# A transducer front end and joint network: a leading tile of 384 outputs, a new load order, and weight sums on other engines

## The chip, the cores and the metric

The kernel runs on one NeuronCore of one Trainium2 chip. A core has five engines that run side by side: TensorE (PE in the profile; its weight loads are shown apart as PEld), VectorE (DVE), ScalarE (ACT), GpSimd (POOL) and SyncE (SP), which here issues DMA transfers. They share an on-chip memory of 128 partitions (SBUF); TensorE writes its products into PSUM, eight banks of 512 fp32 columns a partition. Engines wait for each other through semaphores. The metric is the device time of one execution in microseconds (us); lower is better.

## The reference

Two batches of 4000 steps with 512 channels. A convolution over time with five taps and a 512x512 matrix for each tap, then gelu, then every second step; the same again; then a joint network that adds a projection of each of the 1000 remaining steps to each of eight label vectors, takes tanh and multiplies by a 512x512 matrix. All inputs and the output are bf16.

```python
xp = jnp.pad(x, ((0,0),(2,2),(0,0)))                     # x: (2, 4000, 512)
h = sum(jnp.einsum("btc,cd->btd", xp[:, i:i+4000], w1[i]) for i in range(5))
h = gelu(h)[:, ::2]                                       # (2, 2000, 512)
...                                                       # the same with w2: f is (2, 1000, 512)
fe = jnp.einsum("btd,de->bte", f, w_f)
ge = jnp.einsum("bud,de->bue", g, w_g)                    # 8 label vectors
j = jnp.tanh(fe[:, :, None] + ge[:, None])
return jnp.einsum("btud,dv->btuv", j, w_o)                # (2, 1000, 8, 512)
```

## The kernel before

Channels lie on the partitions: 512 channels are four blocks of 128, so each tap is 4 input blocks by 4 output blocks of 128x128 weights, and time runs along the free dimension. A product is one `matmul` (line 412) of a 128x128 weight block with a run of time steps. Odd outputs of the stride-2 convolution are never computed.

**The leading tile.** The first 2 x `NA` = 408 outputs of batch 0 are computed directly: five taps, 80 products of 408 columns (`direct`, line 691), in the order of taps 0, 4, 2, 1, 3. Tap 0 is cut into two halves of two input blocks each, and tap 4's weights are loaded in two halves, so that work can start early. The x rows for this tile come by two plain loads (`xr`, 128 and 78 rows of four steps) and are transposed by TensorE against an identity matrix into PSUM (`turn`, line 489; 32 transposes); VectorE and ScalarE copy them to `xs`, where four rows hold the four phases of x modulo 4 that the taps pick from. Before x arrives, eight products of 512 columns on a zero tile run on TensorE (`warm_mm`); the zero tile is written by VectorE and is also what the identity matrix is made from.

**The triples.** All other outputs are computed three at a time with fewer products than taps times outputs (`Triple`, line 562, and `Unit`). For each group of columns, one column standing for three outputs, there are nine products (`t2`, `tm`, `sm`, `t1`, `s1`, `t0`, `s0`, `ti`, `si`) of four input blocks each. Their inputs are sums of six phases of x (x modulo 6), made by the steps `d2 d1 d0 t2 r2 r1 tm sm r0 t1 s1 prev s0 next t0 ti si` on ScalarE and VectorE; their weights are sums of taps. The first convolution has four such groups: two for the rest of batch 0 (`N3` = 266 and 266 columns) and two for batch 1 (334 each); the second has two of 334. The six phases come by DMA transposes ("turned" loads, `load_x6`) into `xq` and `xp`.

**The weight sums.** `w1part` (line 542) makes, for each output block of 128, w0+w4-w2, w0+w4+w2 and w0+2 w2+4 w4, the first and the last scaled by a third, and for each pair of blocks w1-w3, w1+w3 and 2 w1. Sums are done on VectorE in fp32 SBUF tiles (`ssum`), scalings on ScalarE.

**The units.** A unit is one output block of one group. It runs its nine products into one of five PSUM banks (4, 5, 6, 7, 3, then 0 to 2 when the leading tile has left them); between products ScalarE copies partial results to `sd`, VectorE combines them in a second bank, and ScalarE writes the gelu.

**The joint stage.** 16000 rows of 512 are multiplied by w_o as a 2x2 block scheme with seven products instead of eight (`Seven`), 31 groups of four 128-row tiles, and one last tile as a plain product in two halves (`end`). ScalarE makes the tanh rows, VectorE and GpSimd make sums of them (`ss`), VectorE and ScalarE bring the products out of PSUM into `sn` and into an output tile `og` of four rows, of which there are three; SP stores them. The two halves of the last tile are stored from ScalarE's queue.

**What sets the order.** The program first lists 1711 operations with what they read and write. The order on each engine is not that of the list: it is a table (`ORDER`, line 69), five strings in which two characters are an operation's number, found beforehand by a planner from assumed costs (the numbers given with each operation; `wire` is the assumed duration of a transfer). Where an operation may run on several engines (`flex`) the table also chooses the engine. Waits follow from the reads and writes. An engine does its work strictly in that order, and the SP queue issues transfers in that order too. A transfer can be given a gate, another load whose landing it waits for:

```python
for i, part, gate in ((0, (lo, al), None), (0, (hi, al), None), (4, (slice(0, NK), slice(0, D // 2)), None),
                      (4, (slice(0, NK), slice(D // 2, D)), 0), (2, None, 1), (1, None, 3), (3, None, 5)):
    load_w1(i, part, gate)
for ph in (4, 0, 2, 1, 3, 5):
    load_xq(0, ph)
```

## Time and profile before

| | us |
|---|---|
| median of three runs | 248.97 (248.63 to 248.98) |
| span of the profiled execution | 247.2 |
| what lies around it (median less span) | 1.77 |
| TensorE busy in the span | 242.8 |
| VectorE, ScalarE, GpSimd busy | 224.8, 210.7, 83.8 |
| first warm-up product, first product of the leading tile | 1.19, 7.37 |

The profiled execution was not timed by itself; its span runs from the first to the last instruction, and the rows of the table set it beside the median of the timed runs. In the profile a row of a timeline is: start, duration, engine, line, operation, output <- inputs, form (partitions x elements), count, and in brackets the idle time of the engine before it and what ended it. A row of the chain of waits is start, duration, what. In a windows row each engine has its busy time and count, then come TensorE's granted clock, the busy share of the DMA engines and GB/s. Products overlap, so the time from one start to the next is what a product costs, and its listed duration is longer. A group row has a count, busy time, mean duration in ns, and idle time before it.

### The profile page before, as it was taken

How to read it: one execution, taken by the hardware profiler on the slowest of the kernel's cores; microseconds unless marked ns; L12 is line 12 of the kernel's file. 1: busy time of each engine (PE TensorE's matmuls, PEld its weight loads, DVE VectorE, ACT ScalarE, POOL GpSimd, SP SyncE). 2: the span in 40 equal slices, each digit the busy share in tenths (PEclk: the TensorE clock that was granted, in tenths of full speed). 3: DMA queues.
4: the chain of work that ended last, by engine and by line, in shares of the span. 5: the costliest groups of instructions: out<-in, count | busy, mean ns of one | idle time of the engine just before them, and what ended most of it. 6: DMA issues, size and time to landing. Idle time of an engine off the chain costs nothing.

```text
span 247.2 us, 5277 instructions
## 1 busy us (share of the span) xinstructions
PE 242.8 (98%) x1932; PEld 186.1 (75%) x1932; DVE 224.8 (91%) x403; ACT 210.7 (85%) x359; POOL 83.8 (34%) x90
## 2 busy tenths in 40 slices
PE   8999999999999999999999999999999999999995
PEld 4657888877666666666567888778788888888883
DVE  1799998867999999699998999999999999999994
ACT  3269799899669857986799999999999999999992
POOL 1000000000000000000015584677887886796861
PEclk9999999999999999999999999999999999999999
DMA  6998999997700340000000234413433655356377
GB/s 215 331 193 168 185 157 205 150 177 174 254 2 3 119 135 3 1 1 3 0 0 3 85 102 139 143 48 129 131 127 103 195 171 172 132 187 200 123 258 233
DMA packets 57890, 31.87 MB, mean 129 GB/s; under 512 B 33835, under 2 KB 57659, under 8 KB 57865
## 3 DMA queue, kind: packets, MB, share of 16 engines
q1 hardware_dynamic: 57577, 31.41, 48.5%
q8 instruction: 15, 0.25, 0.4%
q10 hardware_dynamic: 288, 0.13, 0.2%
q14 instruction: 10, 0.08, 0.1%
HBM read 7.66 MB, written 16.38 MB: 97 GB/s over the span
## 4 chain that ended last, share of the span: by engine, by line
PE 98%; DVE 0%; issue 0%
PE acc L412 97%; PE acc L496 1%; DVE ost L835 0%; DVE xs L505 0%; DVE zero L419 0%
## 5 line engine op out<-in xcount | busy, mean ns | idle before, releaser
L398 DVE TENSOR_TENSOR og<-acc,sn 128x512 bf16<-128x512 f32 x93 | 60.0, 690 | 1.9 <-PE acc L412 1.2
L412 PE MATMUL acc<-tw,ss 128*128 128x256 f16 x372 | 58.0, 273 | 0.0
L404 ACT ACTIVATE jT<-feT,geT 128x1000 bf16<-128x1000 f32 (+6 forms) x56 | 53.2, 1002 | 1.8 <-DVE feT L398 1.5
L834 ACT ACTIVATE sn<-acc 128x512 f32<-128x512 f32 (+1 forms) x70 | 43.0, 707 | 1.0 <-PE acc L412 0.7
L412 PEld LDWEIGHTS acc<-tw,ss 128*128 128x128 f16 x372 | 36.0, 98 | 6.5 <-ACT sn L834 0.2
L903 POOL TENSOR_TENSOR ss<-jT 128x512 f16<-128x512 bf16 x24 | 27.7, 1168 | 25.0 <-DVE feT L398 22.5
L412 PE MATMUL acc<-row,w_sb 128*128 128x334 bf16 (+1 forms) x192 | 31.7, 296 | 0.0
L412 PE MATMUL acc<-wo_sb,jT 128*128 128x256 bf16 x176 | 29.2, 273 | 0.0
L404 ACT ACTIVATE sd<-acc 128x334 f32<-128x334 f32 (+1 forms) x48 | 20.6, 435 | 10.1 <-PE acc L412 9.6
L412 PE MATMUL acc<-row,w_x 128*128 128x266 bf16 (+1 forms) x192 | 28.4, 291 | 0.0
L404 ACT ACTIVATE jX<-feT,geT 128x1000 bf16<-128x1000 f32 (+4 forms) x28 | 27.4, 1042 | 0.0
L394 POOL MEMSET hT<- 128x8 bf16 (+2 forms) x6 | 0.7, 149 | 70.5 <-ACT hT L404 70.5
L412 PEld LDWEIGHTS acc<-row,w_sb 128*128 128x128 bf16 x192 | 18.7, 98 | 6.3
L412 PEld LDWEIGHTS acc<-row,w_x 128*128 128x128 bf16 x192 | 18.7, 98 | 5.7
L903 POOL TENSOR_TENSOR ss<-jT,ss 128x512 f16<-128x512 bf16 x14 | 16.6, 1189 | 15.1 <-DVE ss L903 9.7
L412 PE MATMUL acc<-wo_sb,ss 128*128 128x256 bf16 x124 | 21.0, 273 | 0.0
L412 PEld LDWEIGHTS acc<-wo_sb,jT 128*128 128x128 bf16 x176 | 17.2, 98 | 3.1
L835 DVE COPY sn<-acc 128x512 f32<-128x512 f32 (+1 forms) x25 | 16.8, 691 | 1.1 <-PE acc L412 1.0
L412 PE MATMUL acc<-hT,w_sb 128*128 128x334 bf16 x96 | 17.1, 305 | 0.0
L518 DVE SCALAR_TENSOR_TENSOR acc<-acc,sd 128x334 f32<-128x334 f32 (+1 forms) x24 | 11.7, 487 | 5.8 <-PE acc L412 5.6
L404 ACT ACTIVATE hT<-acc 128x266 bf16<-128x266 f32 (+2 forms) x36 | 14.6, 433 | 2.7 <-PE acc L412 2.4
L834 ACT ACTIVATE og<-acc 128x512 bf16<-128x512 f32 x22 | 15.3, 710 | 1.5 <-PE acc L412 1.5
(113 smaller groups left out, 502.5 us busy)
## 6 DMA issues: line engine op xcount, KB each, us to landing
out_dram<-og SPq DMA_DIRECT2D x45, 256.0 KB, 2.3
w_sb<-in_w_dram SPq DMA_DIRECT2D x8, 512.0 KB, 4.9
out_dram<-og SPq DMA_DIRECT2D x19, 128.0 KB, 2.2
w_sb<-in_w_dram SPq DMA_DIRECT2D x4, 256.0 KB, 4.8
xr<-in_x_dram SPq DMA_DIRECT2D x1, 512.0 KB, 3.5
wf_sb<-in_w_f_dram SPq DMA_DIRECT2D x1, 512.0 KB, 3.6
wg_sb<-in_w_g_dram SPq DMA_DIRECT2D x1, 512.0 KB, 5.1
wo_sb<-in_w_o_dram SPq DMA_DIRECT2D x1, 512.0 KB, 5.2
```

The source lines that it names most:

```text
L394: pl.op("pool", lambda e: e.memset(v.ap, 0.0), (), (v,))
L398: pl.op(eng, lambda e: e.tensor_tensor(out=o.ap, in0=a.ap, in1=b.ap, op=op), (a, b), (o,), 0.02 + 2.14e-3 * o.ap.free_size() if eng == "po ...
L404: pl.op("act", lambda e: e.activation(o.ap, i.ap, func, scale=scale, bias=0.0 if bias is None else bias.ap), rd, (o,), o.ap.free_size() * ...
L412: ins = e.matmul(o.ap, lhsT=l.ap, rhs=r.ap, start=start and n == 0, stop=stop and n == len(pairs) - 1, skip_group_check=not check)
L496: ins = e.transpose(pv.ap[:, i, k, :], xr[rt].h[0:n, 2 * r + pp, k, :], ident.h[0:n, 0:n])
L518: pl.op(eng, lambda e: e.scalar_tensor_tensor(out=o.ap, in0=a.ap, scalar=f, in1=b.ap, op0=ALU.mult, op1=add), (a, b), (o,), vec_cost(o, (a ...
L834: pl.flex({"act": (lambda e: e.activation(o.ap, v.ap, ACT.Copy), 0.05 + n * 0.833e-3), "dve": (lambda e: e.tensor_copy(out=o.ap, in_=v.ap) ...
L835: "dve": (lambda e: e.tensor_copy(out=o.ap, in_=v.ap), 0.065 + n * 1.04e-3)}, (v,), (o,))
L903: fn = lambda e, o=S[i], x=x, y=y, op=op: e.tensor_tensor(out=o.ap, in0=x.ap, in1=y.ap, op=op)
```

## The change

- The leading tile has 384 outputs instead of 408 (`NA` = 192), so the second plain x load has 66 rows; the two groups after it have 206 and 334 columns instead of 266 and 266, and `xq` is sized for the larger one. The turned loads have 224 and 336 columns instead of 272 each.
- The loads on SP: after tap 1 come the turned phases 4 and 0 of the first group, then tap 3, then the other four phases. Tap 3's gate is the first half of tap 4 instead of the second.
- Warm-up products read a constant of the preamble (ones) instead of the zero tile, and the identity matrix is made from a constant; the zero tile and VectorE's write of it are gone.
- Weight sums: ScalarE copies tap 4's block into a PSUM bank, and w0+2 w2+4 w4 is formed there by VectorE. For blocks 0 and 1 w0+w4 also stands in PSUM; for blocks 2 and 3 GpSimd forms w0+w4 and its two sums in SBUF. All four blocks stand in the list ahead of the first group's steps, the sums of w1 and w3 behind them, and those may run on VectorE or GpSimd.
- Copies that scale (steps `d`, `next`, `prev`, and the two `sd` copies of a unit) may run on ScalarE or VectorE (`scaled`).
- The products of the leading tile are no longer kept in the order of the list. The new table runs taps 2 and 1 mixed, and puts tap 3 last with the first `t2` product of the first group ahead of it and two more in between.
- Five output tiles `og` instead of three. The stores of the last group and of the last tile may go on SP's or ScalarE's queue: the table puts two half tiles of the last group and both halves of the last tile on ScalarE's. At the end, the last group's last product comes ahead of both halves of the last tile.
- `ORDER` is new throughout (1718 operations). In it 82 of the partial sums of the joint and feature stages run on GpSimd, 71 before.

```diff
-    NA, N3 = 204, (266, 266)
+    NA, N3 = 192, (206, 334)
...
-        xq = [Buf(nc, f"xq{i}", [6, NK, (288, 288)[i]], BF16, v.end - v.bytes) for i, v in enumerate((xs[1], w2_sb))]
+        xq = [Buf(nc, f"xq{i}", [6, NK, (352, 352)[i]], BF16, v.end - v.bytes) for i, v in enumerate((xs[1], w2_sb))]
...
+        og += [at(f"og{i}", [4, NT], BF16, og_off + (i - 3) * 4096) for i in range(3, 5)]
...
-        pl.op("dve", lambda e: e.memset(zv.ap, 0.0), (), (zv,))
...
-                              (4, (slice(0, NK), slice(D // 2, D)), 0), (2, None, 1), (1, None, 3), (3, None, 5)):
+                              (4, (slice(0, NK), slice(D // 2, D)), 0), (2, None, 1)):
             load_w1(i, part, gate)
-        for ph in (4, 0, 2, 1, 3, 5):
-            load_xq(0, ph)
+        for kind, i in (('w', 1), ('x', 4), ('x', 0), ('w', 3), ('x', 2), ('x', 1), ('x', 3), ('x', 5)):
+            if kind == "w":
+                load_w1(i, None, len(came) - 4)
+            else:
+                load_xq(0, i)
...
+            one = [nc.const_aps.tensor(1.0, [P, k], BF16) for k in (P, NT)]
             for _ in range(n):
-                mm(o, [(z, zz)], True, True)
+                pl.op("pe", lambda e: e.matmul(o.ap, lhsT=one[0], rhs=one[1], start=True, stop=True), (), (o,))
...
+        WBANK = ((6, 7), (5, 4), (6, 7), (5, 4))
+        WHOME = ('P', 'P', 'G', 'G')
+
+        def scaled(o, i, f):
+            n = o.ap.free_size()
+            fast = not i.psum and o.ap.dtype == BF16 and i.ap.dtype == BF16
+            pl.port = fast
+            pl.flex({"act": (lambda e: e.activation(o.ap, i.ap, ACT.Copy, scale=f), n * 0.833e-3 + (0.05 if i.psum else 0.105)),
+                     "dve": (lambda e: e.tensor_scalar_mul(out=o.ap, in0=i.ap, scalar1=f), 0.065 + n * (0.26e-3 if fast else 1.04e-3))}, (i,), (o,))
...
         def w1part(m, part):
...
+            home = WHOME[m]
+            if home != "S":
+                u, t = (ps.cols(bk * NT, NT).map(lambda a: a.rearrange("p (k c) -> p k c", k=NK)) for bk in WBANK[m])
+                act(u, w(4), ACT.Copy)
+                w4 = u
...
+            if home == "G":
+                t, v = ssum[4][:], ssum[m % 2][:]
+                tt("pool", t, w(0), w(4), add)
+                tt("pool", v, t, w(2), sub)
+                tt("pool", w1_t[2, :, sl], t, w(2), add)
+            else:
+                v = t if home == "P" else ssum[m % 2][:]
+                tt("dve", t, w4, w(0), add)
+            stt("dve", u, w4, 4.0, w(0))
+            stt("dve", u, w(2), 2.0, u)
+            act(w1_x[1, :, sl], u, ACT.Copy, scale=1.0 / 3.0)
+            if home != "G":
+                tt("dve", w1_t[2, :, sl], t, w(2), add)
                 tt("dve", v, t, w(2), sub)
+            act(w1_x[0, :, sl], v, ACT.Copy, scale=1.0 / 3.0)
+
+        def w13part(m):
+            n = slice(m * P, (m + 2) * P)
+            shared(w1_x[2, :, n], w1_sb[1, :, n], w1_sb[3, :, n], sub, True)
+            shared(w1_t[0, :, n], w1_sb[1, :, n], w1_sb[3, :, n], add, True)
+            scaled(w1_t[1, :, n], w1_sb[1, :, n], 2.0)
...
-                act(self.c, self.pa(), ACT.Copy, scale=1.5)
+                scaled(self.c, self.pa(), 1.5)
...
+        pl.pin = False
         for i in taps:
...
+        def either(o):
+            o.alt = {"sp": (o.fn, 0.43), "act": (o.fn, 0.43)}
...
-        end.half(0, None, "act")
+        end.half(0, None, None)
         seven[-1].p4()
-        end.half(1, None, "act")
+        end.half(1, None, None)
```

145 lines of the change are left out of this document (69 added, 76 removed).

## The prediction

> **What bounds the kernel now.** I read the page's busy times first, then the chain of waits, then TensorE's timeline.
>
> ```profile
> span 247.2 us, 5277 instructions
> PE 242.8 (98%) x1932; PEld 186.1 (75%) x1932; DVE 224.8 (91%) x403; ACT 210.7 (85%) x359; POOL 83.8 (34%) x90
> ...
> 6.99 0.33 DVE xs L505
> ...
> 7.37 236.76 PE acc L412 x1892
> ...
> 244.15 0.42 DVE ost L835
> ```
>
> The chain is TensorE from 7.37 to 244.13 us without one other engine in it. Ahead of it stands a head of 7.37 us (zeros on VectorE, eight warm-up products, transposes, one eviction), behind it a tail of 247.2 - 244.13 = 3.07 us. So three things can move the time: the head, the length of the product stream, and stalls that a new order makes. Whether the stream is dense shows in runs of equal products:
>
> ```profile
> 21.67 1.54 PE L412 MATMUL acc<-xs,w_sb 128*128 128x408 bf16 x8
> 23.05 2.88 PE L412 MATMUL acc<-row,w_x 128*128 128x266 bf16 x24
> 25.77 2.88 PE L412 MATMUL acc<-xq,w_t 128*128 128x266 bf16 x24
> ...
> 71.44 0.73 PE L412 MATMUL acc<-row,w_sb 128*128 128x334 bf16 x4
> 72.01 0.73 PE L412 MATMUL acc<-xp,w_sb 128*128 128x334 bf16 x4
> ```
>
> From start to start: 408 columns (23.05 - 21.67)/8 = 172.5 ns, 266 columns 2.72/24 = 113.3 ns, 334 columns 0.57/4 = 142 ns. The line through the first two is 0.417 ns a column plus 2.5 ns, and gives 141.7 for the third. There is no stall in it to win back: the 80 + 144 products of the first stages already stand back to back.
>
> **The product stream.** The leading tile goes from 408 to 384 columns in 80 products: 384 gives 162.5 ns, so 80 x 10 = -0.80 us. The two column blocks of the first batch go from 266 and 266 to 206 and 334, with 144 products each: 206 gives 88.3, 334 gives 141.7, so 144 x (88.3 + 141.7 - 226.7) = +0.48 us. Net -0.32 us, on the path in full.
>
> The 206-column product is shorter than any long run shown so far, and each needs its own weights:
>
> ```profile
> L412 PEld LDWEIGHTS acc<-row,w_x 128*128 128x128 bf16 x192 | 18.7, 98 | 5.7
> ...
> 100.92 0.25 PE L412 MATMUL acc<-gT,wg_sb 128*128 128x16 bf16 x4
> 101.02 0.44 PE L412 MATMUL acc<-row,w_t 128*128 128x334 bf16 x2
> ```
>
> A weight load lasts 98 ns, yet four 16-column products with four full loads pass in 0.10 us, 25 ns each: loads follow each other much closer than they last. So 88.3 ns stands. The Trainium skill (TensorE: Matmul & The Clock Gate, Back-to-back issue gap) speaks against it: it says that in a real stream of load and product pairs the spacing is set by both, about 81 ns at 128 columns and 131 at 512. An estimate on the straight line between those two is 91 ns at 206, which would add 0.4 us; the same line gives 117 ns at 408 columns, where this trace has 172.5, so the trace does not agree.
>
> **The head.**
>
> ```profile
> 0.86 0.27 DVE L419 MEMSET zero<- 128x256 uint32 x1 [0.86 <-PEq L1221]
> 1.19 3.59 PE L412 MATMUL acc<-zero 128*128 128x512 bf16 x8 [1.19 <-DVE zero L419]
> 4.27 0.10 PEld L496 LDWEIGHTS acc<-ident,xr 128*128 128x128 bf16 x1 [0.40 <-DMA xr<-in_x_dram]
> 4.58 2.66 PE L496 MATMUL acc<-ident,xr 128*128 128x128 bf16 x32
> ...
> 4.57:6.27 1.70, 1.70 (x16) 1.00 1.03 305
> 6.27:6.78 0.51, 0.51 (x11) 1.00 1.15 333
> 6.78:7.06 0.28, 0.28 (x12) 1.00 1.21 298
> ...
> 6.99 0.92 DVE L505 COPY xs<-acc 128x312 bf16<-128x312 bf16 x2 [0.89 <-PE acc L496]
> ```
>
> The warm-up products wait for VectorE's zeros until 1.19 and run to 4.58, 0.42 us each. With a constant of the preamble as operand they start when the engines do, about 0.86: a gain of 0.33 on their own. But the first transpose also needs x, which lands at 4.27, and the products then end at 4.25; I let the transposes start at 4.33, 0.25 earlier. Sixteen of 128 columns take 1.70 us (106 ns each, half speed by the line above: 55.8; the granted clock, third column of the windows, reads 1.00 all the same). The next eight, of 78 columns, take 0.51 to 6.78, still at half speed; with 66 columns 8 x 55 = 0.44, another -0.07. Only the last eight (0.28) run at full speed. The eviction that releases the first product has 312 elements a row, 0.33 us in the chain, and shrinks with 264 to 0.29. Sum -0.36: the direct products start at 7.0. Bounds: 0 if x lands 0.3 later, -0.45 if the transposes start with x's landing and the fast clock comes a little earlier too.
>
> **Loads: tap 3 behind two turned phases.** One queue (SP) issues everything. Now tap 1, tap 3, then the six phases; after, tap 1, phase 4, phase 0, tap 3, the rest. Three answers on DMA issues, one transfer each (tap 1 issued at 7.08, tap 3 at 8.83 as the second of the same row, phase 4 at 9.24, phase 0 at 10.98), and SP's timeline:
>
> ```profile
> w_sb<-in_w_dram SPq DMA_DIRECT2D x1, 512.0 KB, 5.1
> w_sb<-in_w_dram SPq DMA_DIRECT2D x1, 512.0 KB, 4.8
> xq<-in_x_dram SPq DMA_TRANSPOSE x1, 5.4
> xq<-in_x_dram SPq DMA_TRANSPOSE x1, 6.1
> ...
> 7.08 2.12 SPq L430 DMA_DIRECT2D w_sb<-in_w_dram  x2
> 9.24 1.70 SPq L445 DMA_TRANSPOSE xq<-in_x_dram  x1
> 10.98 2.56 SPq L445 DMA_TRANSPOSE xq<-in_x_dram  x1
> ```
>
> They land at 12.2, 13.6, 14.6 and 17.1: the shares are 1.4 us for a tap, 1.0 and 2.5 for the two phases. The phases shrink from 272 to 224 columns. So after: tap 1 12.2, phase 4 13.0, phase 0 15.1, tap 3 16.5; at the old phase sizes 17.1. SP reaches tap 3's issue at 7.45 + 1.70 + 2.56 = 11.7 at the latest, so the issue is not what is late. TensorE asks for tap 3 after 64 direct products and one group of the triples: 7.0 + 64 x 0.1625 + 4 x 0.088 = 17.8. Cost 0, with 0.7 to 1.3 us to spare. The gate on tap 3 (half of tap 4 landed) is past long before. The phases behind tap 3 land about 1.5 us earlier than now, since they are smaller.
>
> **Weight sums off VectorE's SBUF operands.** Per output block VectorE now does five sums and ScalarE two scalings. After, ScalarE also copies tap 4 into a PSUM bank (four copies); VectorE keeps five sums on PSUM operands for two blocks and two for the other two, whose three remaining sums go to GpSimd.
>
> ```profile
> 7.99 0.69 DVE L398 TENSOR_TENSOR ssum<-w_sb 128x512 f32<-128x512 bf16 x1
> ...
> 10.77 0.69 DVE L518 SCALAR_TENSOR_TENSOR ssum<-w_sb,ssum 128x512 f32<-128x512 bf16 x1 [0.88 <-DMA w_sb<-in_w_dram]
> 11.38 0.69 DVE L398 TENSOR_TENSOR ssum<-ssum,w_sb 128x512 f32<-128x512 f32 x1
> ...
> 13.90 1.15 ACT L404 ACTIVATE w_x<-ssum 128x512 bf16<-128x512 f32 x2 [1.20 <-DVE ssum L518]
> 18.00 0.72 DVE L398 TENSOR_TENSOR row<-xq 128x1064 bf16<-128x1064 bf16 x1
> 18.62 0.69 DVE L518 SCALAR_TENSOR_TENSOR ssum<-w_sb,ssum 128x512 f32<-128x512 bf16 x1
> ...
> L903 POOL TENSOR_TENSOR ss<-jT 128x512 f16<-128x512 bf16 x24 | 27.7, 1168 | 25.0 <-DVE feT L398 22.5
> ```
>
> A 512-element sum is 0.61 from start to start on VectorE, 0.57 on ScalarE, 1.17 on GpSimd; a row sum of 1064 is 0.62, so about 0.50 at 824. PSUM sums with two operands are not in this stage; I take 0.60, between that and the full 0.69. VectorE's first sum starts at 7.99 now, when tap 4's first half is in; with ScalarE's copy ahead it begins at about 8.65 and does in the new order eleven sums (15.25), the first row difference (15.75; phase 0 in at 15.1), three sums (17.5), w1-w3 (18.1), five row steps (20.6), x3-x1 (21.1), x1+x3 (21.6), two more of w1 and w3 (22.8). TensorE wants the first difference at 17.4, x3-x1 at 22.2, the last at 23.9. Everything is 1.0 us or more ahead: cost 0. GpSimd's six sums are 7.0 us; even if all wait for tap 2, which is in by 10.77, they are out by 17.7, and products use them from 22.9 on. At 0.69 a sum, fourteen sums lose 1.3 us and the cover is gone.
>
> **The rest.** The page's waits, a group of the same line on ScalarE's queue, landings, windows, and one stall:
>
> ```profile
> DVE og L398 <- PE acc L412: 1.2, 3, 0.5
> ...
> L849 ACTq DMA_DIRECT2D out_dram<-ost x2: 338/358/378, 244.0 to 244.6; - x2
> ...
> out_dram<-ost ACTq DMA_DIRECT2D x2, 64.0 KB, 2.0
> ...
> 180.00:200.00 20.00, 20.00 (x181) 17.20 (x179) 20.00 (x39) 20.00 (x32) 16.39 (x15) 1.00 0.42 136
> ...
> 241.23 0.33 PEld L412 LDWEIGHTS acc<-tw,jT 128*128 128x128 bf16 x4 [0.19 <-DVE og L398]
> ```
>
> Five output buffers: what writes `og` waits for products today (1.2 us), not for a store, so two more buffers gain 0. Last stores: the chain's end stays product, VectorE eviction 0.42, issue on ScalarE's queue, 2.0 to landing. That queue now carries four stores instead of two at 0.36 each; the one ahead of the last is released one half product (0.44 us) earlier, so it is out in time: 0, between -0.36 and +0.36. The scalings that a planner may now give to VectorE, the warm-up's other operand and the earlier identity matrix cost nothing: their engines have waited for products or x there.
>
> The order of every engine after 30 us is new. I cannot cost it row by row. In the joint stage VectorE and ScalarE are busy for all 20 us of 20, so a bad place costs one late eviction, 0.2 us (the stall shown); a good one removes two such at the end, about -0.1 once the overlap of the weight load is taken off. The order moves eleven of VectorE's partial sums to GpSimd, which has room. Taken: 0, ends -0.2 and +1.0 (five such places).
>
> **Sum.** 247.2 - 0.36 - 0.80 + 0.48 = 246.5 us for the span. The median of the three runs, 248.97, stands 1.77 above the profiled span; I keep that: 248.3 us. Within the forecast the head's and the tail's bounds give 247.8 to 248.7.
>
> **The rivals.** What a measurement of this kernel can tell from no change is about 0.2%, 0.5 us: 248.47 to 249.47.
>
> *Tap 3 late (slower).* Place: the first product of tap 3, at 17.8. The order is fixed, so TensorE stands while the load is out, us for us, and w1-w3 and w1+w3 on VectorE move with it. For: phase 0 alone takes 6.1 us from issue to landing, and if tap 3 took that from 11.7 it would land at 17.8 exactly. Against: it takes 4.8 now, and the shares give 16.5. The gain of 0.68 is gone with a landing at 18.5; from 19.0 it is slower. With 19.7, 1.9 late, the time is 250.2.
>
> *The operands of the first triples late (no change).* Banks 4 to 7 hold sums until ScalarE's scalings, and ScalarE takes its work strictly in order, behind copies that wait for x. For: at 0.69 us a PSUM sum the 1.0 us of room is overdrawn by 0.3, and a phase that lands late holds up all of ScalarE's queue behind its copy. Against: VectorE had the same stage full before without one stall of TensorE. Price 0.2 to 1.1 us: about 249.0.
>
> *The fast clock comes earlier (faster still).* The trace has it at 6.78, 5.6 us after the first product, whatever the reason. If 0.33 us more of early products bring it in by 4.3, the transposes lose 16 x 0.051 + 8 x 0.025 = 1.0 us; the first weights, which land at 6.3 to 6.5 (a load like tap 1's issued at 1.7), cap the gain at 0.6: 247.7. Against: nothing in the trace shows a shorter way to the fast clock. The Trainium skill (TensorE: Matmul & The Clock Gate, The HAM clock gate) has this rule: the clock is released after a busy window of about 3.4 us that runs free of the kernel's start; the 5.6 us here agree with one window that was only partly busy and one full one.
>
> *Weight loads bound (slower).* The change would not give its shorter products: at the load's 98 ns instead of 88.3, 144 products cost 1.4 us: 249.7. Against: 25 ns between loads above.
>
> **How the numbers follow.** Forecast 0.58 (of it 0.10 above 248.47), fast clock early 0.08, operands late 0.18, tap 3 late 0.11, weight loads bound 0.05. Faster 0.48 + 0.08 = 0.56, same 0.10 + 0.18 = 0.28, slower 0.16. The predicted time is the forecast's, 248.3. The range leaves out the end of the early clock below 247.6 and tap 3 landing later than 18.9 above 249.4, under 0.2 together. Since cases of both signs are in it, the forecast's own range is the 247.8 to 248.7 of the sum.
>
> **What would show it.** Right: first warm-up product near 0.86, the direct products from about 7.0 (the chain's last long piece), 162 ns between 384-column products and 88 between 206-column ones, tap 3 down by 17, no wait of TensorE for a load, VectorE or ScalarE up to 35 us, a tail of 3.07. Wrong: a product of `xs` and `w_sb` waiting for the load of `w_sb` near 17.8; products of `row` waiting for VectorE or ScalarE from 20 to 25; GpSimd sums well over 1.2 us between 9 and 17; transposes starting no earlier than 4.58; more stalls of the kind shown at 241.23 in the joint stage.

## The result and the profile after

The changed kernel takes 251.22 us (median of four runs, 250.93 to 251.62) against 248.81 us for the kernel before beside it (248.63 to 248.98): a ratio of 1.0095, with a 95% interval of 1.0082 to 1.0107. It is slower by 2.4 us. The forecast was 248.3 us, 247.6 to 249.4.

The first rows of the page, and its rows of the stores (KB each, median us from issue to landing). The page of the kernel before has 45 stores of 256 KB at 2.3 us.

```profile
span 249.5 us, 5277 instructions
...
PE 242.3 (97%) x1932; PEld 183.1 (73%) x1932; DVE 226.1 (91%) x404; ACT 198.3 (79%) x344; POOL 103.6 (42%) x111
...
out_dram<-og SPq DMA_DIRECT2D x45, 256.0 KB, 2.8
```

The span is 2.3 us longer, TensorE is busy for half a microsecond less, and the stores take longer to land. The timeline of the changed kernel, engine by engine (start, duration, engine, line, operation, form, count, and in brackets the idle time before and what ended it), shows the head, tap 3's place, a run of 206-column products, TensorE's end, and the last work of ScalarE and SyncE:

```profile
0.77 3.31 PE L486 MATMUL acc<-const-bfloat16-1.0 128*128 128x512 bf16 x8 [0.77 <-PEq L1256]
4.20 1.07 PE L499 MATMUL acc<-ident,xr 128*128 128x128 bf16 x16
6.67 1.63 PE L413 MATMUL acc<-xs,w_sb 128*128 128x384 bf16 x9 [0.53 <-DMA w_sb<-in_w_dram]
...
17.11 0.52 PE L413 MATMUL acc<-row,w_x 128*128 128x206 bf16 x4
17.69 2.12 PE L413 MATMUL acc<-xs,w_sb 128*128 128x384 bf16 x12
19.65 0.87 PE L413 MATMUL acc<-row,w_x 128*128 128x206 bf16 x8
21.00 2.29 PE L413 MATMUL acc<-row,w_x 128*128 128x206 bf16 x24
23.12 0.52 PE L413 MATMUL acc<-xq,w_t 128*128 128x206 bf16 x4
...
243.62 1.04 PE L413 MATMUL acc<-wo_sb,jT 128*128 128x256 bf16 x8
...
243.05 2.86 ACTq L1001 DMA_DIRECT2D out_dram<-og  x1
246.01 0.60 ACT L869 ACTIVATE og<-acc 128x512 bf16<-128x512 f32 x1 [2.42 <-DVE ost L870]
246.47 1.00 ACTq L884 DMA_DIRECT2D out_dram<-ost  x2
...
243.14 0.90 SPq L991 DMA_DIRECT2D out_dram<-og  x2
244.24 2.77 SPq L1001 DMA_DIRECT2D out_dram<-og  x2
```

Three stretches account for the 2.3 us:

- **Head.** The first direct product starts at 6.67 instead of 7.37: 0.70 us gained. Sixteen transposes take 1.07 us, where the first sixteen took 1.70 before: TensorE ran at full speed by 4.2, before only from 6.78. This compares one execution with one; other executions of the same head follow further down.
- **Stream.** From there to the last product it is 237.99 us (244.66 less 6.67) against 236.74 before: 1.25 us lost. The products themselves are as short as forecast: twelve of 384 columns start in 1.96 us (19.65 less 17.69), 163 ns each, and 24 of 206 columns in 2.12 us, 88 ns each. So 0.32 us was gained, and TensorE must stand 1.57 us more.
- **Tail.** From the last product to the end of the span it is 4.84 us (249.5 less 244.66) against 3.07 before: 1.77 us lost.

Together: -0.70 + 1.25 + 1.77 = 2.3 us.

Where TensorE stands is in the view of waits, from 7.5 to 246 us, for its products and its weight loads (us in total, times, longest). The kernel before has no row for its products there, and five rows of 0.2 to 0.4 for its loads:

```profile
PE acc L413 <- DVE og L399: 0.6, 1, 0.6
...
PEld acc L413 <- DVE og L399: 1.6, 4, 0.8
PEld acc L413 <- ACT jT L405: 0.6, 2, 0.4
PEld acc L413 <- DVE sn L870: 0.4, 1, 0.4
PEld acc L413 <- DMA w_sb<-in_w_dram: 0.3, 1, 0.3
```

Part of a load's wait is covered by the product ahead of it. Measured between the starts of products, the standing is 0.23 us at 17.4 (tap 3), 0.21 at 123.3 (the first tanh rows), 0.13 at 189.8 and about 1.3 between 210.4 and 214.3: 1.87 us. With all the smaller gaps, reckoned as start-to-start time beyond 0.417 ns a column and 2.5 ns, it is 2.18 us here and 0.61 in the kernel before: the 1.57 us more.

**The standing at 210** is VectorE's, and VectorE stands for stores. SyncE, VectorE and TensorE in the timeline around it:

```profile
201.15 1.64 SPq L884 DMA_DIRECT2D out_dram<-og  x3
204.99 2.23 SPq L991 DMA_DIRECT2D out_dram<-og  x4
...
208.46 0.68 DVE L870 COPY sn<-acc 128x512 f32<-128x512 f32 x1
210.50 2.48 DVE L399 TENSOR_TENSOR og<-acc,sn 128x512 bf16<-128x512 f32 x4 [1.36 <-PE acc L413]
...
211.25 0.39 PE L413 MATMUL acc<-wo_sb,jT 128*128 128x256 bf16 x2 [0.57 <-DVE og L399]
```

The bracket blames a product that had long been done. Each eviction into an `og` buffer waits for the store that emptied it, and the order table says which. The first three stores of the 204.99 row, worked out from the trace: when the last eviction that fills the block ended, when SyncE issued the store, when it landed.

```
block          data ready   issued    landed
og2, upper     204.96       204.99    207.80
og0, upper     198.31       205.41    209.69
og4, upper     195.28       205.92    210.38
```

Two stores whose data had been there for 7 and 11 us stood in SyncE's list behind one whose data came at 204.96, while SyncE did nothing from 202.8 to 205.0. The eviction that starts at 210.50 goes into og4's upper half. The same reckoning for all stores on SyncE's queue after 60 us: before, 94 stores wait 0.5 us on the average between data and issue, none over 3.0; after, 92 wait 3.7 us, 40 of them over 3.0, the longest 20.0.

**The tail.** ScalarE issues a half store at 243.05 and this takes 2.86 us; the eviction of the last group's lower left block is next in its list and starts at 246.01 instead of about 243.7, and the last stores follow it.

### The profile page after: what moved, and what is told of

It reads as the page before. It is cut to its first block, busy times and chain, and to the rows that moved or that the text cites. A ratio compares the mean times of both kernels' runs of the same rounds, so it can differ in the third digit from the quotient of the medians.

```text
span 249.5 us, 5277 instructions
## 1 busy us (share of the span) xinstructions
PE 242.3 (97%) x1932; PEld 183.1 (73%) x1932; DVE 226.1 (91%) x404; ACT 198.3 (79%) x344; POOL 103.6 (42%) x111
## 4 chain that ended last, share of the span: by engine, by line
PE 88%; DMA 4%; SPq 2%; DVE 2%; issue 1%; ACT 1%; ACTq 0%; DVEq 0%
PE acc L413 88%; DMA w_sb<-in_w_dram 4%; SPq L444 2%; DVE feT L399 1%; DVE og L399 1%; ACT jT L405 0%; DVE ost L870 0%; SPq L437 0%; ACTq L1001 0%; DVE sn L870 0%; ACT og L869 0%; SPq L457 0%; SPq L429 0%; DVE tw L588 0%; DVEq L245 0%
## 5 line engine op out<-in xcount | busy, mean ns | idle before, releaser
L405 ACT ACTIVATE jT<-feT,geT 128x1000 bf16<-128x1000 f32 (+6 forms) x56 | 51.8, 971 | 0.3 <-DVE feT L399 0.3
L550 ACT ACTIVATE sd<-acc 128x334 f32<-128x334 f32 (+1 forms) x39 | 16.2, 426 | 19.3 <-PE acc L413 16.4
L943 POOL TENSOR_TENSOR ss<-jT 128x512 f16<-128x512 bf16 x23 | 26.7, 1174 | 6.7 <-ACT jT L405 5.6
L413 PE MATMUL acc<-row,w_x 128*128 128x334 bf16 (+1 forms) x192 | 29.2, 292 | 0.0
L405 ACT ACTIVATE jX<-feT,geT 128x1000 bf16<-128x1000 f32 (+4 forms) x28 | 25.4, 934 | 0.0
L943 POOL TENSOR_TENSOR ss<-jT,ss 128x512 f16<-128x512 bf16 x16 | 18.6, 1172 | 7.8 <-DVE ss L943 7.4
L405 ACT ACTIVATE hT<-acc 128x334 bf16<-128x334 f32 (+2 forms) x36 | 14.7, 430 | 3.2 <-PE acc L413 3.2
L413 PE MATMUL acc<-row,w_t 128*128 128x334 bf16 x96 | 16.6, 305 | 0.0
L413 PE MATMUL acc<-xp,w_t 128*128 128x334 bf16 x96 | 16.2, 305 | 0.0
L943 POOL TENSOR_TENSOR ss<-jX 128x512 f16<-128x512 bf16 x13 | 15.1, 1168 | 1.1 <-PE acc L413 1.1
```

The lines of the kernel that those rows point to most:

```text
L405: pl.op("act", lambda e: e.activation(o.ap, i.ap, func, scale=scale, bias=0.0 if bias is None else bias.ap), rd, (o,), o.ap.free_size() * ...
L413: ins = e.matmul(o.ap, lhsT=l.ap, rhs=r.ap, start=start and n == 0, stop=stop and n == len(pairs) - 1, skip_group_check=not check)
L550: pl.flex({"act": (lambda e: e.activation(o.ap, i.ap, ACT.Copy, scale=f), n * 0.833e-3 + (0.05 if i.psum else 0.105)), "dve": (lambda e: e ...
L943: fn = lambda e, o=S[i], x=x, y=y, op=op: e.tensor_tensor(out=o.ap, in0=x.ap, in1=y.ap, op=op)
```

## The experiments

Theory A: the half store on ScalarE's queue holds back the last eviction, and the tail is its doing. Theory B: the order in which SyncE issues its stores makes both the standing at 210 and a backlog at the end. The rivals were an operand late for other reasons at 210, and stores that are slow to land by themselves.

### Taking the two queue edits apart

```diff
 e1: ScalarE: ... evict og4 lower
-    store half (1,1); evict (1,0); store half (0,0); store ost, store ost
+    evict (1,0); store ost, store ost
     SyncE, its end:
+    store half (1,1) ahead of og3 lower, store half (0,0) ahead of half (0,1)
 e2: ScalarE:
-    store half (1,1); evict (1,0); store half (0,0)
+    evict (1,0); store half (1,1); store half (0,0)
 e3: SyncE: all stores sorted by the time their data was ready; ScalarE as changed
 e4: e3, and the half stores on SyncE's queue
```

> The changed kernel with its two half-group stores taken off ScalarE's queue and put back among SyncE's last stores; nothing else differs. Theory A (the half store that ScalarE issued for 2.86 us, 243.05 to 245.91, held back the eviction of the last group's lower half queued behind it, and with it three of the last stores): that eviction starts at about 243.65 to 244.1, the last stores of the ost halves are issued by about 245.5, and the end comes 1.2 to 2.0 us earlier, 249.2 to 250.0 us. Theory B (the tail is late because SyncE's stores of the whole last part are behind, and each store takes its place in that backlog whoever issues it): the end stays within 0.4 us of 251.2, since SyncE then has two stores more behind the same backlog. The 1.3 us that TensorE stands at 210 to 214 stays in both.

> The changed kernel with the eviction of the last group's lower half put ahead of the half store on ScalarE's list, so that nothing but stores is queued behind the long issue. If the issue is long because ScalarE's queue gets no turn before the backlog of SyncE's stores is gone (about 246.4), the half store is still finished at about 246, the three behind it follow at 0.4 to 0.6 each, and the end stays within 0.5 us of 251.2. If the 2.86 us belong to the first store of that queue, whenever it is issued, it runs 244.7 to 247.6 and the end comes at 252.0 to 253.0. If only the eviction's place mattered, the end comes 1.0 us or more earlier.

> The changed kernel with SyncE's stores sorted by the time at which their data was ready in its own trace; the two half stores stay on ScalarE's queue. The theory that the stores out of their order make the 1.3 us of TensorE's standing at 210 to 214 (the stores of og0 and og4 ready at 198.3 and 195.3 were issued at 205.4 and 205.9, behind one whose data came at 205.0, and VectorE waited for their landing at 209.7 and 210.4): that standing goes, 1.0 to 1.3 us. If the backlog is also what made ScalarE's first issue 2.86 us, that issue falls below 1 us and the end gains 1.2 to 2.0 us more: 248.0 to 249.0 us in all. If the long issue belongs to ScalarE's queue, only the first gain comes: 249.9 to 250.3. Rival: the stall at 210 is TensorE's own order (an operand late from GpSimd or ScalarE), then it stays and the time is 250.5 or more.

> Stores sorted by readiness and the half stores on SyncE's queue too. If the order of the stores and the long issue are the two losses and they add up, 247.9 to 248.8 us, under the kernel before by 0 to 0.9 us; if the sorted order alone already shortens the issue on ScalarE's queue, the same time as with the sorting alone within 0.4 us.

Measured, beside 248.81 us for the kernel before: e1 250.70 us (ratio 1.0077, 1.0049 to 1.0105), e2 250.91 (1.0088, 1.0057 to 1.0119), e3 250.09 (1.0054, 1.0033 to 1.0076), e4 249.68 (1.0035, 1.0023 to 1.0046).

The late eviction in the timeline of e1:

```profile
243.60 0.60 ACT L869 ACTIVATE og<-acc 128x512 bf16<-128x512 f32 x1 [0.22 <-PE acc L413]
```

The eviction starts 2.4 us sooner, as theory A says, but the time falls by only 0.5 us, where A wanted 1.2 to 2.0 and B up to 0.4. With the eviction ahead of the stores (e2) it also starts at 243.75, and the time falls by 0.3, inside the half microsecond of the first of its three cases. So the eviction was late, and cheap: most of the tail lies elsewhere.

Sorting the stores (e3) is worth 1.13 us. That is the second band, and not the rival. The standing at 210 is gone: VectorE's four evictions there, and the whole view of TensorE's waits for them, in e3:

```profile
208.89 2.51 DVE L399 TENSOR_TENSOR og<-acc,sn 128x512 bf16<-128x512 f32 x4
...
PEld acc L413 <- DVE og L399: 0.2, 1, 0.2
```

That settles what the standing at 210 was. The stores are not slow by themselves either: in e3 those of 256 KB land in 2.2 us (median), as in the kernel before (2.3) and not as in the changed one (2.8). But e3 keeps the long issue, so the sorted order does not shorten it, and the larger gain that was tied to that did not come:

```profile
241.53 2.90 ACTq L1001 DMA_DIRECT2D out_dram<-og  x1
244.53 0.60 ACT L869 ACTIVATE og<-acc 128x512 bf16<-128x512 f32 x1 [2.45 <-DVE ost L870]
```

The two edits add up to 1.54 us in e4 (1.13 + 0.41), where 2.4 to 3.3 were expected, and 0.9 us of the loss are left.

### The half stores alone, on the kernel before

```diff
-                pl.dma("sp", lambda e: e.dma_start(dst, src.ap), ...)
+                pl.dma("act" if r == c else "sp", lambda e: e.dma_start(dst, src.ap), ...)
```

with the same places in ScalarE's list as in the changed kernel.

> The kernel before with one part of the change alone: the same two half stores on ScalarE's queue, the first ahead of the last group's lower eviction, as in the changed kernel. If ScalarE's queue by itself makes the issue of 128 KB long (2.9 us in the changed kernel, also with the stores sorted), that eviction starts at about 246 instead of 243.7 and the time is 250.2 to 251.0 us. If the long issue needs the queue of SyncE's stores that the changed order piles up, it takes 0.4 to 0.9 us here and the time stays within 0.3 us of 248.8.

249.23 us against 248.77 (1.0016, 1.0005 to 1.0027): 0.4 us slower, just outside what the second case allowed. ScalarE's first issue is short here:

```profile
242.93 0.43 ACTq L959 DMA_DIRECT2D out_dram<-og  x1
243.60 0.60 ACT L834 ACTIVATE og<-acc 128x512 bf16<-128x512 f32 x1 [1.24 <-PE acc L412]
```

So ScalarE's queue is not slow by itself, and the edit still costs 0.4 us here, about what moving it back saved in e1 and e4.

### What is left of the tail

In e4 the last product ends at 243.05, 1.06 us earlier than in the kernel before, and yet the last store lands at 247.10, 4.05 us later, against 2.47 before. Two runs put the order of the kernel before back: e5 from the first output product on, e6 for the last 80 products, on top of e4. One run (e12) keeps the new order and draws the closing products of earlier blocks forward.

```diff
 e5: all engines, from the first output product on: the order of the kernel before
 e6: e4, and the last 80 products with what hangs on them in the order of the kernel before
 e12: e4, and in the last 84 products those that close a block of an earlier group up to 14 places sooner
 e13: e12, and one second-convolution product ahead of the first output product
```

> The changed kernel up to its first output product; from there on, on all five engines and on SyncE's queue, the written order of the kernel before (the half stores on SyncE's queue again with it). The leading tile, the loads, the weight sums and the five group buffers stay as changed. If the new order of the output part is where the loss is (the 1.3 us at 210 to 214, the 2 us of the tail, the 0.2 us at 123), the time is the one before less the head (0.70) and the stream (0.32) plus the stall on tap 3 (0.23): 248.0 us, 247.7 to 248.4. If the loss comes with the leading tile or the five buffers, it stays above 250.

> The kernel of the two queue edits together (stores by readiness, half stores on SyncE's queue) with the last 80 products and all that hangs on them in the order of the kernel before. There TensorE ended at 243.05 and the last store landed at 247.10, 4.05 us later, against 2.47 us in the kernel before (244.11 to 246.58). If the rest of the loss is that the new order finishes the blocks of the last three groups late and in a bunch (five stores of 128 to 256 KB issued after 241.4), the wait after the last product falls back to 2.5 to 3.0 us and the time to 248.1 to 248.8 us. If the order of products has no part in it (the stores just take longer to land), it stays at 249.4 to 249.9.

> The kernel of the two queue edits together, with the last 84 products, and the evictions, sums and stores that hang on them, put in another order: the products that finish a block of an earlier group come up to 14 places sooner (those of the third- and fourth-last groups above all), and the last group's closing products five places sooner; engines, amounts of work and the order before 222 us are the same. If the 4.05 us between the last product and the last landing (2.47 in the kernel before) are the order in which the last groups' blocks come ready, they fall to 3.0 to 3.6 us and the time to 248.9 to 249.4 us. If they are the stores' own slowness or the two stores more on SyncE's queue, the time stays within 0.2 us of 249.7.

> The same with one more move: a product of batch 1's second convolution (0.57 us, the one that ran behind the first four output products at 124.3) put ahead of the first output product, for which TensorE waited 0.22 us at 123.2 in the changed kernel (that product's tanh came at 123.65 there). If that wait is a matter of the order alone it goes, with 0.2 us of the time; if what follows waits as much later, no change against the run without it.

Measured: e5 253.63 us (1.0208, 1.0158 to 1.0258), e6 250.27 (1.0049, 1.0029 to 1.0068), e12 252.27 (1.0134, 1.0101 to 1.0166), e13 251.93 (1.0124, 1.0105 to 1.0143). As times e5, e6 and e12 are misses, and e13 stays within the noise of e12. The wait behind the last product is shorter in all: 2.7 us in e5, 2.9 in e6, 3.0 in e12. That alone does not show that the order of products sets it, since the last product also ends later (248.85, 246.09 and 245.99 us against 243.05 in e4) and the stores had that time to go out. Each order brought new standing of TensorE with it, e5 and e6 at the seam between the two orders, e12 in the last 24 us. The longest rows of e5 from 120 to 135 us, then of e12 from 222 on:

```profile
PEld acc L414 <- ACT sd L551: 3.3, 1, 3.3
```

```profile
PEld acc L413 <- DVE og L399: 2.5, 6, 1.0
PEld acc L413 <- ACT sn L869: 1.0, 3, 0.4
```

In e13 the wait at 123 did not go; it moved to 125.2 (0.25 us there instead of 0.21). It was not a matter of one product's place.

A whole order can't be exchanged cheaply, so e15 moves one block. In e4 SyncE's 256 KB store of og3's lower half is issued at 241.87, 1.2 us ahead of the last product's end; in the kernel before the store at the same place in the groups was issued 4.1 us ahead. The cause in the table: the two half products that close it stand nine places apart, in the kernel before they are neighbours.

```diff
 e15: e4, and in TensorE's order
-    1670, 1661, 1683, 1684, 1689, 1687, 1700, 1690, 1701, 1671, 1696
+    1670, 1671, 1661, 1683, 1684, 1689, 1687, 1700, 1690, 1701, 1696
     its eviction one place sooner on ScalarE, its store four places sooner on SyncE
 e16: e15 with the two half stores on ScalarE's queue, behind its last eviction
 e17: e15 with the last group's upper row in one store
```

> The kernel of the two queue edits together (249.68 us) with one block moved: the second half product of the third-last group's lower right block stands right behind its first half (eight places sooner, as in the kernel before, where the two are neighbours), its eviction one place sooner on ScalarE, where 1.5 us lay idle ahead of 240.0, and its store of 256 KB ahead of the next group's three. If the tail is long because whole stores come ready in a bunch in the last 2 us, this store goes out at about 240.2 instead of 241.9, the four behind it move up by 0.4 to 0.5 us, and the wait after the last product falls from 4.05 to 2.9 to 3.5 us: 248.5 to 249.2. If it is the bytes of the last 4 us as a whole, not the place of one store, the time stays within 0.2 us of 249.7.

> The same, with the two half stores on ScalarE's queue behind its last eviction. If a store on ScalarE's queue is issued slowly only while many of SyncE's stores are still to be moved, and there are fewer now, its first issue takes 0.4 to 0.9 us and the time is that of the run without this edit within 0.3 us. If SyncE's stores of the last 2 us are enough to hold it (1.7 us in the run with the eviction first), the first issue takes over 1.2 us and the time is 0.3 to 1.2 us longer than without.

> The kernel with the one block moved (249.00 us), and the last group's upper row stored as one store of 256 KB when both halves are there (242.8) instead of two of 128 KB. If the end is set by SyncE's last stores being issued one behind the other (four from 241.6 to 244.4, each 0.4 to 0.6 us, while the data of the last was there at 242.9), one store fewer brings the last issue and the last landing 0.3 to 0.5 us forward, to 248.5 to 248.8 us, at or under the kernel before. If the bytes set it, the half that now waits 0.6 us for its neighbour takes that gain back and the time stays within 0.15 us of 249.0.

e15: 249.00 us (1.0012, 1.0001 to 1.0024), 0.68 less than e4. SyncE's last stores in e4, then in e15:

```profile
241.43 0.39 SPq L1001 DMA_DIRECT2D out_dram<-og  x1
241.87 1.40 SPq L991 DMA_DIRECT2D out_dram<-og  x2
243.32 1.57 SPq L1001 DMA_DIRECT2D out_dram<-og  x3
```

```profile
237.82 2.29 SPq L991 DMA_DIRECT2D out_dram<-og  x3
...
241.62 0.65 SPq L1001 DMA_DIRECT2D out_dram<-og  x1
242.31 0.47 SPq L991 DMA_DIRECT2D out_dram<-og  x1
242.82 1.56 SPq L1001 DMA_DIRECT2D out_dram<-og  x3
```

The store has joined the row that starts at 237.82 (it goes out at 239.74), and the last three follow 0.5 us sooner. The last landing is at 246.42, 3.29 us behind the last product, which ends at 243.13 as in e4: what was expected of a bunch of whole stores, and here the shorter wait is not bought with a later product. e16: 249.25 us (1.0021, 1.0011 to 1.0030), within 0.3 us of e15, with a first issue of 0.92 us. e17: 248.87 us against 248.94 (0.9996, 0.9981 to 1.0012), inside the band expected of "the bytes set it" as much as near the other; its last landing comes 3.0 us behind the last product. The interval does not tell e17 from e15, so what the last 0.5 us of the tail consist of stays open.

So the loss is walked back in steps: 251.22, 250.09 (stores sorted), 249.68 (half stores on SyncE's queue), 249.00 (one block), 248.87 (one store fewer). The last is the kernel before's time; none beats it.

### The head and the first stage

```diff
 e8, on the kernel before:
-                mm(o, [(z, zz)], True, True)
+                pl.op("pe", lambda e: e.matmul(o.ap, lhsT=one[0], rhs=one[1], start=True, stop=True), (), (o,))
 e9, on the kernel before; e10: e8 and e9:
-    NA, N3 = 204, (266, 266)
+    NA, N3 = 192, (206, 334)
-        xq = [Buf(nc, f"xq{i}", [6, NK, (288, 288)[i]], ...
+        xq = [Buf(nc, f"xq{i}", [6, NK, (352, 352)[i]], ...
 e18: e9, and
-        memset(xq[1][0:4, :, 1 + N3[1]:4 + N3[1]])
-        memset(xq[1][4:6, :, N3[1]:4 + N3[1]])
+        for ph in (4, 0, 2, 1, 3, 5):
+            memset(xq[1][ph, :, (1 if ph < 4 else 0) + N3[1]:4 + N3[1]])
 e11 and e14, on e4:
-        for kind, i in (('w', 1), ('x', 4), ('x', 0), ('w', 3), ...
+        for kind, i in (('w', 1), ('w', 3), ('x', 4), ('x', 0), ...      # e11
+        for kind, i in (('w', 1), ('x', 4), ('w', 3), ('x', 0), ...      # e14
```

> The kernel before with one part of the change alone: the warm-up products read constant operands and not the zeroed tile, so they wait for no memset. If the earlier start of the products (1.19 to 0.77 us) is the whole of the head's gain, the first direct product comes at 6.65 to 6.95 instead of 7.37 and the time falls by 0.4 to 0.7 us, to 248.1 to 248.4; if the gain needs the other edits of the head, under 0.2 us.

> The kernel before with one part of the change alone: the leading tile of 384 outputs and parts of 206 and 334 (192 pairs, 352-column buffers) instead of 408 and 266/266; loads, warm-up, weight sums, three group buffers, the written order and the stores stay as before. If the stream's term of the forecast stands by itself, the products take 0.32 us less and the time is 248.3 to 248.6. If the wider second part makes VectorE or a phase load late under the old order, TensorE stands for 0.3 us or more in the first stage and the time is the same or longer, 248.7 to 249.5.

> The leading tile of 384 outputs and the warm-up on constants together, on the kernel before. If both gains are real and add, 248.1 to 248.5 us; if the first stage goes at the pace of its loads (the warm-up alone brought the direct products 0.97 us forward in its profile and only 0.08 us in the time), no more than the tile alone within 0.15 us.

> The kernel before with the tile of 384 outputs and, as the change has it, the columns behind the second group's run zeroed phase by phase (six small writes of GpSimd) instead of two writes over several phases. In the run with the tile alone VectorE stood 1.95 us at 32.3 for the second of these writes, which waited for the last phase (34.06), and TensorE 2.7 us behind it; the time was 4.0 us over the kernel before. If that wait is what the tile alone was missing, it goes, with 2.5 to 2.9 us: 249.9 to 250.6. If the rest (VectorE's rows and ScalarE's scalings late at 19.8 to 29.3, 1.6 us by the waits) also comes from the two writes, 248.3 to 248.7; if the old order keeps the stage late whatever is zeroed, 252 or more.

> The kernel of the two queue edits together (249.68 us) with tap 3 loaded ahead of the two turned phases again. If the wait on tap 3 (0.23 us at 17.4 in the changed kernel, tap 3 landing at 17.64) costs what it shows, it goes and the time falls by 0.1 to 0.3 us. If the turned phases are then late for the first triple, TensorE stands elsewhere before 25 us and the time stays or rises.

> The kernel of the two queue edits together (249.68) with tap 3 loaded between the two turned phases, where the changed kernel has it behind both and the run with tap 3 ahead of both took 250.88. If the first triple waits for its second phase (x0) as it did there, about half of that loss or all of it: 250.1 to 250.9. If only the first phase (x4) decides, 249.4 to 249.8.

e8: 248.69 us against 248.77 (0.9996, 0.9986 to 1.0006). In its profile the head is 0.97 us shorter:

```profile
0.77 3.19 PE L484 MATMUL acc<-const-bfloat16-1.0 128*128 128x512 bf16 x8 [0.77 <-PEq L1222]
6.40 1.90 PE L412 MATMUL acc<-xs,w_sb 128*128 128x408 bf16 x10 [0.34 <-DMA w_sb<-in_w_dram]
```

In the time it is worth less than can be measured. In the same profile TensorE stands 0.26 us at 22.9 and 0.1 at 27.7, where the kernel before does not: both times it waits for VectorE's sums of a row, which come about half a microsecond earlier where TensorE comes 0.97 earlier. So 0.55 us is left at the last product (243.56 against 244.11). That the ten timed runs show 0.08 us is the second case's band, under 0.2, though not its reason: in this execution the head itself did get shorter.

e9: 252.91 us (1.0139, 1.0115 to 1.0162), far over both bands. The tile alone loses 4.0 us, and 2.7 of it at one place. GpSimd and VectorE there:

```profile
34.11 0.13 POOL L394 MEMSET xq<- 128x32 bf16 x1 [2.67 <-DMA xq<-in_x_dram]
...
34.27 0.85 DVE L398 TENSOR_TENSOR row<-xq 128x1336 bf16<-128x1336 bf16 x1 [1.95 <-POOL xq L394]
```

One small write zeroes the columns behind the run in two phases at once, so it waits for the last phase to land, and VectorE's sums of an earlier phase wait for the write. The change writes phase by phase; I had not seen that this carries weight. With it (e18) the time is 250.63 (1.0068, 1.0051 to 1.0084), 0.03 over the first band: the wait at 32 us falls from 2.7 to 0.7, and the rest stays. TensorE's waits for VectorE and ScalarE in e18 from 15 to 40 us:

```profile
PEld acc L412 <- DVE row L398: 1.5, 3, 0.8
PEld acc L412 <- ACT w_x L404: 0.4, 1, 0.4
```

The changed kernel has none of these rows. So the tile's 0.32 us are not to be had with the old loads, weight sums and order of the first stage, whose change was costed at nothing; which of the three the tile needs was not taken apart. e10 (254.41 us, 1.0197, 1.0159 to 1.0235) adds the earlier warm-up to the tile and is 1.5 us slower than e9. In its profile TensorE comes earlier to the same late stage, stands 3.09 us at 32 us instead of 2.52, and its products then run at half speed for about 6 us (last section). The two of its six runs with a mean granted clock of 1.0 took 251.83 and 253.21 us, no longer than e9's.

e11: 250.88 us against 249.68 for e4 (1.0072 over the kernel before, 1.0058 to 1.0086). e14: 251.04 us (1.0085, 1.0067 to 1.0102). With tap 3 ahead of the second phase TensorE waits for the first triple (e11, weight loads from 15 to 36 us):

```profile
PEld acc L413 <- DVE row L399: 0.7, 2, 0.4
PEld acc L413 <- ACT sd L550: 0.5, 1, 0.5
PEld acc L413 <- ACT w_x L405: 0.3, 1, 0.3
```

The time rises by 1.2 us. Placed between the phases tap 3 costs as much (0.14 us over the first band), so the second phase (x0) decides: it lands at 13.38 us in e4, at 16.22 in e11 and at 17.06 in e14. There was no wait on tap 3 to win back: e4, on which both are built, shows none, and neither do e1, e3 and e15, with the same loads; in the changed kernel it is 0.23 us, in e2 0.32, in e17 0.11. The late tap is the cheaper of the two: at most 0.32 us against 1.2.

## Why the prediction was wrong, point by point

The step that failed is the term for the new order, taken as 0 with +1.0 us at most and sized by late evictions alone, together with the step on the output buffers that let a store stand unnoticed. The runs showed in its place that SyncE's list of stores costs 1.13 us by its order (e3) and 0.68 us by one block that comes late in the tail (e15), and that the half stores on ScalarE's queue, also taken as 0, cost 0.4 to 0.5 us (e1, e4, e7).

- **The product stream, -0.32 us.** Right: 163 and 88 ns between products, and 0.32 us over the whole stream.
- **Weight loads as the bound.** Did not happen: no wait of that kind at 206 columns.
- **The head, -0.36 us.** In the profile 0.70. The first product comes at 0.77, not 0.86, and the rival "the fast clock comes earlier" happened in the shown execution: full speed by 4.20. It brought little: the products start at 6.67 because TensorE then waits for the second x load (0.20) and the first weights (0.53), and in e1 and e3, where the 32 transposes take 2.37 and 2.34 us, they start at 6.71. How much of the 0.70 is this execution's luck can only be bounded: in the fourteen profiles with the changed kernel's head the first direct product comes at 6.28 to 7.47, median 6.69; with the old head and tile it is 7.37 and, in e7, 7.24. What the forecast missed is that a head read from one execution need not show in the time (e8: 0.08 us). In the profiles of the new order it does reach TensorE's end: the last product ends 1.06 us (e4) and 0.98 us (e15) earlier than before, of which the head is 0.75 and 0.77.
- **Tap 3, 0 us, landing at 16.5 with room to 17.8.** It landed at 17.64, over the upper estimate of 17.1, and with the head earlier TensorE asked at 17.46: 0.23 us of standing, which e1, e3, e4 and e15 do not have. The rival "tap 3 late" had the place right, but took it to be 1.9 us late. The load takes 5.7 us here, 5.1 or 4.8 in the rows that the estimate came from. The forecast's 0 for the first triple's operands holds, but only through this edit (e11).
- **Weight sums, 0 us with 1.0 us of room.** Right in the changed kernel; e18 shows about 2 us lost with the old loads, sums and order under the new tile (250.63 against 248.99 us, and the 0.32 not gained).
- **Five output buffers, 0 us: "what writes `og` waits for products today, not for a store".** This step failed. Even its reading left out a row of the kernel before's waits, one for a store: `DVE og L398 <- DMA out_dram<-og: 0.3, 1, 0.3`. No run has the buffers alone, so their own worth is not shown. With five the table left a store for up to 20 us, and once the stores are out of their order, what writes `og` does wait for a store. I looked at the buffers' users and not at the queue that empties them.
- **The new order, 0 us, ends -0.2 and +1.0.** This term was the largest error. I sized it by late evictions at 0.2 us each, and left SyncE's list out of it. Its stores' order is worth 1.13 us (e3), one block's place in the tail 0.68 (e15), the waits at 123 and 189, which no run took away, 0.34: about 2 us, twice the upper end.
- **Last stores on ScalarE's queue, 0 us within 0.36.** The step's reason ("the one ahead of the last is released earlier, so it is out in time") fell: the first of them took 2.86 us to issue, and the eviction queued behind it waited 2.4. I named nothing that stands behind that issue. Its price is small all the same: 0.4 to 0.5 us (e1, e4, e7), little over the bound.

The sum in these terms: -0.32 for the stream and about -0.6 for the head; +1.13 for the stores' order, +0.41 for the queue (e4 against e3), +0.68 for the block, +0.34 for the waits at 123 and 189; what e17 took off the tail, +0.13, and what its tail still is over the kernel before's, +0.54 (3.01 against 2.47 us). Together +2.3 of the +2.4 measured, where the forecast had 0 for all but the first two. The last two are not explained.

## What to carry to other kernels

An in-order queue of stores is a resource like an engine: when buffers are added or an order is planned anew, compare for each store when its data is ready and when it is issued, because one store in front whose data comes late holds back all that stand behind it, and through the buffers the engines that refill them. Which blocks become ready last moves the tail, so finish whole blocks early and leave small pieces for the end. An edit that looks like a loss by itself (here tap 3's load put later) may be what pays for another one, and a gain at the head that one execution shows need not show in the time (e8).

## What the runs showed of the hardware

**An issue on ScalarE's queue can take 2.9 us.** The first half store there took 2.86 us in the changed kernel, 2.90 in e3, and 0.43 in e7, the same 128 KB. SyncE's stores issued in the meantime took 0.4 to 0.9 each. In the changed kernel the first packet of ScalarE's queue runs at 246.41, half a microsecond after the issue's end. What holds the issue was not settled: sorting the stores left it, and in e16 it took 0.92 us. The traces hold a nearer candidate than SyncE's stores, a packet of 8 KB in a queue that the page calls "instruction". In the changed kernel it starts at 243.81, inside the long issue; e7 has none from 240.5 to 246.5 us. The changed kernel's row (packets, MB, share of the DMA engines) in that stretch:

```profile
q14 instruction: 1, 0.01, 0.9%
```

In the nine profiles in which ScalarE's first store takes 0.87 us or more to issue (the changed kernel, e1 to e4, e6, e11, e14, e16) the issue ends 1.5 to 2.1 us after such a packet starts. In the other eleven it takes 0.37 to 0.44 us, and the last such packet started about 1.6 us or more ahead of it. That fits ScalarE waiting for its own next instructions, and then the shorter issue of e16 owes nothing to fewer stores. It is not shown: the trace does not say for which engine the packet is, and no run moved it alone. The Trainium skill (DMA: Bandwidth & Descriptors, Issuing engines are not separate DMA queues) says that issuing from several engines only saves the sequencer's issue time, usually small; here a second queue saved no time and lost 0.4 us.

**TensorE ran at half speed after standing for 2.9 us.** In e5 it waited 2.93 us and then ran for 3.3 us at a granted clock of 0.51 (products of 334 columns 279 ns apart instead of 142). In e10 it waited 3.09 us, and the clock was 0.50 from 35.6 to 41.5 us; in e9, after 2.52 us, it stayed at 1.00. The timeline's row and the clock by stretches of e5, then a stretch of e10 (PE, PEld, DVE, ACT and POOL busy, then the clock, DMA share, GB/s):

```profile
129.16 1.30 PE L414 MATMUL acc<-hT,w_sb 128*128 128x334 bf16 x4 [2.93 <-ACT sd L551]
...
129.00:132.30 3.30, 3.15 (x13) 1.88 (x14) 0.66 (x2) 1.12 (x2) 0.00 (x0) 0.51 0.00 0
132.50:135.00 2.50, 2.50 (x20) 1.83 (x19) 1.83 (x6) 0.32 (x1) 0.00 (x0) 1.00 0.00 0
...
35.60:41.50 5.90, 5.86 (x25) 3.65 (x26) 4.41 (x7) 2.82 (x6) 0.00 (x0) 0.50 1.04 179
```

The Trainium skill (TensorE: Matmul & The Clock Gate, Part 1: The HAM clock gate) has the slow state come after an idle window of about 3.4 us; here stands a little shorter than that were enough, and the slow state lasted about as long as that window in e5 and nearly twice as long in e10.
